# Row norms of an attention stage: sums of squares in four column tiles, and the factors spread by DMA instead of by TensorE

## The chip, the cores and the metric

The kernel runs on one core of a Trainium2 chip. The metric is device time in microseconds (us), first to last instruction of one execution, median of several. Five engines work side by side and each runs its own instructions in the order in which they were written: TensorE (PE; its weight loads stand in the trace as PEld), VectorE (DVE), ScalarE (ACT), GpSimd (POOL) and SyncE (SP). In this kernel SP issues every DMA, so a DMA that waits for its data holds back all DMAs written behind it. Matmul results land in PSUM, in banks of 512 fp32 values per partition.

## The reference

Three stages, fp32 throughout. For 8 batches, 8 heads, 576 tokens and head size 64:

```python
p_packed = sm_attn(p, k, v)              # 32 packed queries per head
out = sm_attn(q, p_packed, p_packed)     # 576 tokens per head over 32 packed rows
x = out.transpose(0, 2, 1, 3).reshape(4608, 512)

rms = np.sqrt(np.mean(x * x, axis=-1, keepdims=True) + 1e-06)
xn = x / rms * rms_g                     # the norm that the change is about
g = xn @ w_gate                          # 512 x 1536
silu = g * (1.0 / (1.0 + np.exp(-g)))
x = silu * (xn @ w_val) @ w_out          # 1536 x 512

h = (x @ w1) * (x @ w2) @ w3             # 512 x 1024, 1024 x 1024
return h @ w_out2                        # 1024 x 512
```

## The kernel before

The first 500 us hold the attention and the gated layer, batch by batch; the rest holds the output products, which the change doesn't touch.

**Attention.** `pack(b)` (line 182) makes the packed rows of a batch, `unpack(b)` (line 256) the second attention and the row norm. Neither multiplies its attention weights by the packed rows: what leaves `unpack` is `a2T`, the softmax weights with the 32 packed rows of four heads on the 128 partitions, two such halves `e`, and 576 tokens in the free dimension. The packed rows are folded into the gate and value weights instead (`wb_unit`, line 349). So the sum of squares of a token's output row is taken through the 32x32 Gram matrices `G` of the packed rows: `sq` = (G a2T) * a2T (lines 305 to 317), the halves added on POOL (line 319), and then summed over the 128 partitions. Lines 323 to 339 do that sum and what follows: five matmuls with `sq` as the stationary operand and a 128x2 tile of ones moving, so that tokens come out on partitions; one DVE instruction that scales it (`ssq`); two small POOL instructions (+1e-6, power -0.5, giving `rinv`, 128 partitions x 5); five TensorE transposes of `rinv`, each column repeated 128 times, which put the 576 factors on every partition; and two DVE products that scale `a2T` with them. `ah` and `al` are the high and low fp32r halves of the result, split by ACT (`ah`) and DVE (`al`).

**Dense units.** `dense_units(b)` (line 382) is the gated layer: 48 units for a batch, each of six matmuls of 288 tokens into one of four PSUM banks named `gv`. Units come in pairs. After the first of a pair ACT takes a tanh (`th`, line 402) and DVE a product (line 403), which frees the bank; after the second ACT copies the bank (`vl`, line 407, two buffers) and POOL multiplies (`ht`, line 408, three buffers). Every four units one `ht` is stored to `hT_d` by SP. After units 3, 11, 19, 27, 35 and 43 `wb_unit` makes the next folded weights in eight matmuls (line 358), which ACT and DVE split into `wbh` and `wbl` (lines 59, 60).

**What sets the order.** The schedule is manual: `planned` runs a batch's dense units and, after unit n, one step (up to a `yield`) of each other generator for each time that n stands in its list. While the units of batch b run, `UNPACK` places the 18 steps of `unpack(b+1)`, `PACK` the 7 steps of `pack(b+2)`, and a third list the conversions of 64-bit weights (`convert`, lines 115 to 121, and a 512 KB load each). All small products take their PSUM from two alternating slots named `at`. In this text a step of `unpack` is U1, U2, ..., a step of `pack` P1, P2, ...; U13 is the sum over partitions, U14 the two POOL instructions, U15 and U16 the two scalings, U17 and U18 the splits. P4 (line 219) is followed by the load of the next `v` (`vt`, 1 MB and 128 KB). `pack` runs beside the units of batches 0 to 5 and loads `vt` beside those of 0 to 4; `unpack` of batches 1 to 7 runs beside those of 0 to 6, and `unpack(0)` before the first unit.

Of the kernel before, what the change touches and what calls it, by code (L numbers as in the profile page):

```python
# [8 lines left out]
F32 = mybir.dt.float32  # L9
# [23 lines left out]
def packed_attention_swiglu_bilinear(ctx: ExitStack, tc, qT, kT, v, v_end, pT, rms_g, w_gv, w_out,  # L33
                                     w1, w2, w3T, w_out2, out):
    nc = tc.nc
# [16 lines left out]
    def slot(tag):  # L52
        return slots.tile([128, 2, 512], F32, tag=tag, name=tag, bufs=2)
# [8 lines left out]
    ident = const.tile([128, 128], F32, name="ident")  # L62
# [6 lines left out]
    att = att_ctx.enter_context(tc.tile_pool(name="att", bufs=1, side="left"))  # L69
# [95 lines left out]
    wgv = wraw.tile([128, NC, 2, DFF], F32, name="wgv")  # L165
    bdP1T = att.tile([128, 2, NC, 2, NP], F32, name="bdP1T")
    G = att.tile([128, 2, 2, NP], F32, name="G")
    mhalf = att.tile([128, R], F32, name="mhalf")
    ones = att.tile([128, 2], F32, name="ones")
    nc.gpsimd.memset(ones, 1.0)  # L170
    nc.gpsimd.memset(mhalf, -0.5)
    nc.gpsimd.memset(bdP1T, 0.0)
# [4 lines left out]
    def place(c, e):  # L177
        return 32 * ((c + e) % NC)

    def pack(b):  # L180
# [7 lines left out]
        for a in range(2):  # L188
            for c in range(NC):
                for e in range(2):  # L190
                    e0 = slice(64 * e, 64 * e + 64)
                    nc.tensor.matmul(ts[e][32 * c:32 * c + 32, a, :HALF], lhsT=pTs[e0, c, b],
                                     rhs=ks[e0, c, HALF * a:HALF * a + HALF],
                                     start=True, stop=True, tile_position=(64 * e, 32 * c))
# [60 lines left out]
    def unpack(b):  # L255
# [12 lines left out]
        for a, t in enumerate(ts):  # L268
            for c in range(NC):
                for e in range(2):  # L270
                    e0 = slice(64 * e, 64 * e + 64)
                    r = place(c, e)
                    nc.tensor.matmul(t[r:r + 32, e, :HALF], lhsT=bdP1T[e0, b % 2, c, e, :],
                                     rhs=qs[e0, c, HALF * a:HALF * a + HALF],
                                     start=True, stop=True, tile_position=(64 * e, r))
        for a, t in enumerate(ts):
            nc.vector.transpose(out=a2.rearrange("p e t n -> p e (t n)")[:, :, HALF * a:HALF * a + HALF],
                                in_=t[:, :, :HALF])
# [25 lines left out]
        sq = att.tile([128, 2, S], F32, tag="sq", name="sq")  # L304
        ts = [slot("at") for _ in range(2)]
        for a in range(2):
            for e in range(2):
                for c in range(NC):
                    r = place(c, e)
# [3 lines left out]
                                     rhs=x[:, HALF * a:HALF * a + HALF],  # L313
                                     start=True, stop=True, tile_position=(k, r))
        for e in range(2):
            nc.vector.tensor_tensor(out=halves(sq[:, e]), in0=ts[e][:, :, :HALF], in1=halves(a2T[:, e]),
                                    op=ALU.mult)
            yield
        nc.gpsimd.tensor_tensor(out=sq[:, 0], in0=sq[:, 0], in1=sq[:, 1], op=ALU.add)
        yield  # L320
        ssq = att.tile([128, R], F32, tag="ssq", name="ssq")
        rinv = att.tile([128, R], F32, tag="rinv", name="rinv")
        t = slot("at")
        for r in range(R):
            nc.tensor.matmul(t[:, 0, 2 * r:2 * r + 2], lhsT=sq[:, 0, T0[r]:T0[r] + 128], rhs=ones,  # L325
                             start=True, stop=True, skip_group_check=True)
        nc.vector.tensor_scalar(out=ssq, in0=t[:, 0, :2 * R].rearrange("p (r j) -> p r j", j=2)[:, :, 0],
                                scalar1=0.0, scalar2=1.0 / DM, op0=ALU.max, op1=ALU.mult)
        yield
        nc.gpsimd.tensor_scalar(out=ssq, in0=ssq, scalar1=1e-6, scalar2=None, op0=ALU.add)  # L330
        nc.gpsimd.tensor_tensor(out=rinv, in0=ssq, in1=mhalf, op=ALU.pow)
        yield

        t = slot("at").rearrange("p a n -> p (a n)")
        for r in range(R):
            nc.tensor.transpose(t[:, 64 + T0[r]:192 + T0[r]], rinv[:, r:r + 1].to_broadcast([128, 128]), ident)
        for e in range(2):
            nc.vector.tensor_tensor(out=a2T[:, e], in0=a2T[:, e], in1=t[:, 64:64 + S], op=ALU.mult)
            yield
        ah = dp.tile([128, 2, S], F32R, tag="ah", name="ah", bufs=2)  # L340
        al = dp.tile([128, 2, S], F32R, tag="al", name="al", bufs=2)
        for e in range(2):
# [139 lines left out]
    for n in range(16):  # L482
        r, c = GROUPS[n // 4]
        w, kk = ((w1, r), (w1, r + 2), (w2, r), (w2, r + 2))[n % 4]
        jobs.append((w[128 * kk:128 * kk + 128, 512 * c:512 * c + 512], w12_d[n]))
    ow = converting(jobs, out_weight)

    PACK = [7, 7, 16, 31, 32, 40, 43]
    UNPACK = [0, 1, 3, 4, 6, 11, 13, 15, 17, 24, 24, 25, 31, 32, 40, 41, 42, 44]
    for b in range(B - 1):  # L490
        others = [(UNPACK, unpack(b + 1))]
        if b + 2 < B:
            others.insert(0, (PACK, pack(b + 2)))
# [567 lines left out]
```

## Time and profile before

| | us |
|---|---|
| median of 3 runs | 1362.85 (1362.68 to 1364.24) |
| the profiled execution | 1364.01 |
| its span, first to last instruction | 1361.9 |
| PE busy in the span | 1310.4 (96%) |
| DVE, POOL, ACT busy | 846.9, 607.5, 571.9 |
| mean granted TensorE clock | 0.985 |

The profile says for each engine when an instruction ran, how long, and what ended the wait before it. A busy PE isn't proof of a full PE, since matmuls overlap. Two views tell more: the timeline, where the distance from one start to the next is the time an instruction takes up, and the list of waits, where an engine that sets the pace has next to none. The first 107 us are start-up; from there to 500 us the dense units follow each other.

### The profile page before, as it was taken

The numbers are of one execution on the slowest core, as the hardware profiler recorded it, in microseconds if no ns is written. First come the engines' busy times: TensorE is split into PE (matmuls) and PEld (weight loads), VectorE is DVE, ScalarE is ACT, GpSimd is POOL, SyncE is SP. The second block draws the span as 40 slices with busy tenths as digits, with TensorE's granted clock in tenths as the row PEclk, the third lists the DMA queues.
The fourth block names the chain that finished last, engine by engine and source line by source line (L and its number), as shares of the span: only waits on it lengthen the run. The fifth ranks groups of instructions, "written<-read, shape, count | busy, mean of one in ns | idle before, by whom it ended". The sixth has DMA issues, their size and how long they took to land.

```text
span 1361.9 us, 23336 instructions
## 1 busy us (share of the span) xinstructions
PE 1310.4 (96%) x8824; PEld 1108.8 (81%) x8824; DVE 846.9 (62%) x1284; ACT 571.9 (42%) x1093; POOL 607.5 (45%) x524
## 2 busy tenths in 40 slices
PE   4589999999999999999999999999999999999998
PEld 2367888788888888888888888888888888899998
DVE  5787676776766557736376564567468457557444
ACT  3465565566656665625244342025005103304113
POOL 2466555466556552212132123447345545535543
PEclk9589999999999999999999999999999999999999
DMA  8755656575353467744299984656755855787875
GB/s 328 289 176 167 232 188 241 175 239 165 121 176 127 155 198 253 238 131 135 84 348 369 344 295 176 249 208 212 279 194 206 277 207 195 247 316 254 280 268 188
DMA packets 88704, 304.01 MB, mean 223 GB/s; under 512 B 9872, under 2 KB 14992, under 8 KB 74384
## 3 DMA queue, kind: packets, MB, share of 16 engines
q1 hardware_dynamic: 88592, 302.52, 63.5%
q8 instruction: 69, 1.13, 0.3%
q14 instruction: 43, 0.35, 0.1%
HBM read 223.87 MB, written 76.55 MB: 221 GB/s over the span
## 4 chain that ended last, share of the span: by engine, by line
PE 84%; DVE 5%; POOL 2%; issue 2%; DMA 2%; ACT 1%; SPq 0%; ACTq 0%; DVEq 0%; POOLq 0%
PE gv L396 19%; PE gv L896 13%; PE at L896 13%; PE at L583 12%; PE gv L583 7%; PE gv L990 5%; PE at L990 5%; PE gv L684 3%; PE at L358 3%; POOL sl L60 1%; DVE c_t L118 1%; DVE wgv L119 1%; PE at L325 1%; DMA hT_d<-ht 1%; DVE th L403 1%
## 5 line engine op out<-in xcount | busy, mean ns | idle before, releaser
L408 POOL TENSOR_TENSOR ht<-th,vl 128x288 f32<-128x288 f32 x192 | 162.5, 854 | 122.4 <-ACT vl L407 47.4
L396 PE MATMUL gv<-ah,wbh 128*128 128x288 f32 x768 | 175.1, 309 | 2.9 <-ACT vl L407 2.4
L396 PE MATMUL gv<-ah,wbl 128*128 128x288 f32 x768 | 165.2, 296 | 2.3 <-DVE wbl L60 2.3
L396 PEld LDWEIGHTS gv<-ah,wbh 128*128 128x128 f32 x768 | 121.9, 190 | 54.2 <-issue 24.5
L396 PE MATMUL gv<-al,wbh 128*128 128x288 f32 x768 | 165.0, 296 | 0.0
L60 DVE TENSOR_TENSOR hl<-hr,hh 128x512 fp32r<-128x512 f32 x108 | 100.0, 933 | 78.8 <-ACT hh L59 76.7
L922 POOL TENSOR_TENSOR s<-uc 128x512 f32<-128x512 f32 (+1 forms) x40 | 48.9, 1223 | 217.9 <-DVE uc L878 217.9
L121 POOL TENSOR_TENSOR c_o<-c_o,c_y 128x512 int32<-128x512 int32 x52 | 70.8, 1361 | 152.4 <-DVE c_o L119 114.2
L896 PE MATMUL gv<-xh,w 128*128 128x512 f32 (+1 forms) x560 | 137.9, 368 | 0.0
L896 PE MATMUL at<-xh,w 128*128 128x512 f32 (+1 forms) x560 | 137.8, 368 | 0.0
L396 PEld LDWEIGHTS gv<-ah,wbl 128*128 128x128 f32 x768 | 123.7, 189 | 3.4 <-DVE wbl L60 3.3
L396 PEld LDWEIGHTS gv<-al,wbh 128*128 128x128 f32 x768 | 124.0, 189 | 0.0
L403 DVE SCALAR_TENSOR_TENSOR th<-th,gv 128x288 f32<-128x288 f32 x192 | 84.9, 444 | 59.8 <-ACT th L402 43.2
L59 ACT ACTIVATE hh<-hr 128x512 fp32r<-128x512 f32 x108 | 67.8, 630 | 117.3 <-PE at L583 61.1
L896 PEld LDWEIGHTS gv<-xh,w 128*128 128x128 f32 x560 | 102.6, 188 | 13.4
L407 ACT ACTIVATE vl<-gv 128x288 f32<-128x288 f32 x192 | 78.9, 411 | 82.1 <-PE gv L396 49.4
L896 PEld LDWEIGHTS at<-xh,w 128*128 128x128 f32 x560 | 102.5, 188 | 13.2
L583 PE MATMUL at<-hh,wo_l 128*128 128x512 f32 x288 | 112.2, 390 | 0.0
L583 PE MATMUL at<-hl,wo_h 128*128 128x512 f32 x288 | 112.2, 390 | 0.0
L583 PE MATMUL at<-hh,wo_h 128*128 128x512 f32 x288 | 112.2, 390 | 0.0
L402 ACT ACTIVATE th<-gv 128x288 f32<-128x288 f32 x192 | 79.2, 413 | 43.5 <-PE gv L396 41.6
L60 POOL TENSOR_TENSOR xl<-yi,xh 128x1024 fp32r<-128x1024 f32 (+1 forms) x20 | 55.1, 2757 | 71.7 <-ACT xh L59 47.8
(158 smaller groups left out, 2790.6 us busy)
## 6 DMA issues: line engine op xcount, KB each, us to landing
w<-ws_d SPq DMA_DIRECT2D x40, 1024.0 KB, 4.9
w<-w_d SPq DMA_DIRECT2D x35, 1024.0 KB, 4.8
w<-ws_d SPq DMA_DIRECT2D x40, 768.0 KB, 5.1
hT_d<-ht SPq DMA_DIRECT2D x96, 288.0 KB, 4.0
hr<-hT_d SPq DMA_DIRECT2D x108, 256.0 KB, 4.8
w<-in_w_gv_dram SPq DMA_DIRECT2D x24, 512.0 KB, 6.8
w<-in_w_out_dram SPq DMA_DIRECT2D x20, 512.0 KB, 6.1
q<-in_qT_dram SPq DMA_DIRECT2D x8, 1152.0 KB, 7.1
```

The costliest lines, as they stand in the source:

```text
L59: nc.scalar.activation(out=hi, in_=src, func=AF.Copy)
L60: eng_lo.tensor_tensor(out=lo, in0=src, in1=hi.bitcast(F32), op=ALU.subtract)
L121: nc.gpsimd.tensor_tensor(out=d, in0=d, in1=shape(y), op=ALU.add)
L396: nc.tensor.matmul(t[:, :HALF], lhsT=w[:, e, 256 * i + 128 * f:256 * i + 128 * f + 128], rhs=x[:, e, HALF * hf:HALF * hf + HALF], start=(n ...
L402: nc.scalar.activation(out=th, in_=t[:, :HALF], func=AF.Tanh, scale=0.5)
L403: nc.vector.scalar_tensor_tensor(out=th, in0=th, scalar=1.0, in1=t[:, :HALF], op0=ALU.add, op1=ALU.mult)
L407: nc.scalar.activation(out=vl, in_=t[:, :HALF], func=AF.Copy, scale=0.5)
L408: nc.gpsimd.tensor_tensor(out=ht[:, hf], in0=th, in1=vl, op=ALU.mult)
L583: nc.tensor.matmul(acc[m], lhsT=w[:, kk, 128 * m:128 * m + 128], rhs=x, start=(kk == 0 and a == 0), stop=(kk == NF - 1 and a == 2))
L896: nc.tensor.matmul(t, lhsT=wi[:, r, pos, a], rhs=x[:, j, r, :w], start=(start and at == 0), stop=(at == 5), skip_group_check=True)
L922: nc.gpsimd.tensor_tensor(out=s2, in0=u2, in1=c22, op=ALU.mult)
L990: nc.tensor.matmul(t, lhsT=wi[:, s, k, 128 * m:128 * m + 128], rhs=x, start=(j in (0, 5, 4, 3) and k == 0 and n == 0), stop=(k == 3 and n ...
```

## The change

For batches 1 to 7 the sum over partitions, the power and the spread are made in another way; batch 0 keeps the old code under `if b == 0`.

- The five matmuls with `sq` stationary become four with a 128x32 tile of ones stationary and 144 tokens of `sq` moving each. They are set side by side in the array's columns (`tile_position=(0, 32 * c)`) and write 32 equal rows each into one bank.
- DVE scales 128x144 values instead of 128x5 (`sums`). Four DMAs take one row of each group of 32 and lay it out on 24 partitions, 6 tokens each (`ssq`, 96x6).
- POOL's two instructions work on 96x6; a DMA stores the factors in DRAM (`rinv_d`), and another reads them back to all 128 partitions (`rb`, 128x576, in the buffer of `turned`). The five transposes are gone. The two scalings read `rb` from SBUF.
- `unpack` has 19 steps instead of 18 for these batches (the read of `rb` is one by itself), and the lists of places are new, for the conversions too.

```diff
-        t = slot("at")
-        for r in range(R):
-            nc.tensor.matmul(t[:, 0, 2 * r:2 * r + 2], lhsT=sq[:, 0, T0[r]:T0[r] + 128], rhs=ones,
-                             start=True, stop=True, skip_group_check=True)
...
-        t = slot("at").rearrange("p a n -> p (a n)")
-        for r in range(R):
-            nc.tensor.transpose(t[:, 64 + T0[r]:192 + T0[r]], rinv[:, r:r + 1].to_broadcast([128, 128]), ident)
-        for e in range(2):
-            nc.vector.tensor_tensor(out=a2T[:, e], in0=a2T[:, e], in1=t[:, 64:64 + S], op=ALU.mult)
-            yield
...
+            t = slot("at")
+            for c in range(4):
+                nc.tensor.matmul(t[32 * c:32 * c + 32, 0, :Q4], lhsT=ones, rhs=sq[:, 0, Q4 * c:Q4 * c + Q4],
+                                 start=True, stop=True, tile_position=(0, 32 * c), skip_group_check=True)
+            nc.vector.tensor_scalar(out=sums, in0=t[:, 0, :Q4], scalar1=0.0, scalar2=1.0 / DM, op0=ALU.max, op1=ALU.mult)
+            for c in range(4):
+                nc.sync.dma_start(out=ssq[24 * c:24 * c + 24], in_=sums[32 * c:32 * c + 1].rearrange("p (a n) -> p a n", n=6))
+            yield
+            nc.gpsimd.tensor_scalar(out=ssq, in0=ssq, scalar1=1e-6, scalar2=None, op0=ALU.add)
+            nc.gpsimd.tensor_tensor(out=rinv, in0=ssq, in1=mhalf[:96], op=ALU.pow)
+            nc.sync.dma_start(out=rinv_d[b], in_=rinv)
+            yield
+            nc.sync.dma_start(out=rb, in_=rinv_d[b].rearrange("p n -> (p n)").partition_broadcast(128))
+            yield
+            for e in range(2):
+                nc.vector.tensor_tensor(out=a2T[:, e], in0=a2T[:, e], in1=rb, op=ALU.mult)
+                yield
...
-    PACK = [7, 7, 16, 31, 32, 40, 43]
-    UNPACK = [0, 1, 3, 4, 6, 11, 13, 15, 17, 24, 24, 25, 31, 32, 40, 41, 42, 44]
+    PACK = [6, 7, 18, 32, 34, 41, 47]
+    UNPACK = [0, 0, 3, 3, 7, 12, 14, 17, 17, 25, 26, 26, 30, 32, 35, 40, 40, 40, 42]
...
-            others.append(([9, 20, 28, 35, 46], some(ow, 5)))
+            others.append(([8, 19, 22, 31, 44], some(ow, 5)))
```

New lines shift the old ones: line 396 (the dense matmuls) becomes 421, line 219 becomes 221, 403 becomes 428, 60 becomes 62. In the rows below a name is what an instruction writes, then what it reads; "x2" counts equal neighbours.

On PE, where the sum over partitions stands, in a batch before:

```order
L396 MATMUL gv<-ah,wbl 128x288 x2
L219 MATMUL at<-vt,a1T 32x64 x40
L325 MATMUL at<-ones,sq 128x2 x5
L396 MATMUL gv<-ah,wbh 128x288 x2
L396 MATMUL gv<-al,wbh 128x288 x2
```

and after (line 350 is the new sum):

```order
L421 MATMUL gv<-ah,wbl 128x288 x2
L350 MATMUL at<-sq,ones 32x144 x4
L421 MATMUL gv<-ah,wbh 128x288 x2
L421 MATMUL gv<-al,wbh 128x288 x2
L421 MATMUL gv<-ah,wbl 128x288 x2
L421 MATMUL gv<-ah,wbh 128x288 x2
L421 MATMUL gv<-al,wbh 128x288 x2
L421 MATMUL gv<-ah,wbl 128x288 x2
L221 MATMUL at<-vt,a1T 32x64 x40
L421 MATMUL gv<-ah,wbh 128x288 x2
```

The sum stood behind P4 without a dense unit between them; now two units lie between, and the sum comes first.

On SP, at the same place (`w` is a weight load, `vt` the next batch's v, `wo_d` a converted weight), before:

```order
L106 DMA w_1957<-in_w_out_dram 128x1024
L376 DMA hT_d<-ht 128x576
L97 DMA vt<-in_v_dram 128x2048
L98 DMA vt<-in_v_end_dram 64x512
L376 DMA hT_d<-ht 128x576
```

and after:

```order
L354 DMA ssq<-sums 24x1x6 x4
L108 DMA w_2015<-in_w_out_dram 128x1024
L99 DMA vt<-in_v_dram 128x2048
L100 DMA vt<-in_v_end_dram 64x512
L358 DMA rinv_d<-rinv 96x6
L401 DMA hT_d<-ht 128x576
L360 DMA rb<-rinv_d 128x576
L401 DMA hT_d<-ht 128x576
```

The six new DMAs stand around the weight load and the load of `vt`, with an `ht` store behind each of the last two.

On DVE, around the scaling of `a2T` (`bdP1T`, `gP1T` and `G` belong to `pack`), before:

```order
L235 COPY bdP1T<-at 64x4x32 x2
L237 TENSOR_TENSOR gP1T<-at,gT 128x128
L338 TENSOR_TENSOR a2T<-a2T,at 128x576 x2
L403 SCALAR_TENSOR_TENSOR th<-th,gv 128x288
L60 TENSOR_TENSOR al<-a2T,ah 128x576
L249 COPY G<-at 128x64
L60 TENSOR_TENSOR wbl<-at,wbh 128x1024
L403 SCALAR_TENSOR_TENSOR th<-th,gv 128x288
```

and after:

```order
L363 TENSOR_TENSOR a2T<-a2T,rb 128x576 x2
L62 TENSOR_TENSOR al<-a2T,ah 128x576
L237 COPY bdP1T<-at 64x4x32 x2
L239 TENSOR_TENSOR gP1T<-at,gT 128x128
L428 SCALAR_TENSOR_TENSOR th<-th,gv 128x288
L62 TENSOR_TENSOR al<-a2T,ah 128x576
L62 TENSOR_TENSOR wbl<-at,wbh 128x1024
L428 SCALAR_TENSOR_TENSOR th<-th,gv 128x288
L120 TENSOR_SCALAR c_t<-c_h 128x512
L121 SCALAR_TENSOR_TENSOR c_o<-c_h,c_t 128x512
L428 SCALAR_TENSOR_TENSOR th<-th,gv 128x288
L266 COPY G<-at 128x64
```

The first split and the copies of P6 now stand between the scaling and the next `th` product, and the copy of `G` (P7) has moved behind a weight's conversion.

## Rows read from the trace of the kernel before

**Rows 1.** The page, busy time, share and instructions; then the stage 272 to 327 us.

```profile
PE 1310.4 (96%) x8824; PEld 1108.8 (81%) x8824; DVE 846.9 (62%) x1284; ACT 571.9 (42%) x1093; POOL 607.5 (45%) x524
...
272.00:327.00 55.00, 54.11 (x603) 45.23 (x602) 40.35 (x75) 34.29 (x75) 33.31 (x37) 1.00 0.60 203
```

**Rows 2.** Waits of PE from 100 to 500 us: total, times, longest.

```profile
PE gv L396 <- DVE wbl L60: 2.3, 4, 0.9
```

**Rows 3.** Timeline of PE at P4 and the sum: start, us, line, [idle].

```profile
275.98 0.42 PE L396 MATMUL gv<-ah,wbl 128*128 128x288 f32 x2
276.33 1.32 PE L219 MATMUL at<-vt,a1T 128*32 128x64 f32 x80
277.58 1.28 PE L325 MATMUL at<-ones,sq 128*128 128x2 f32 x10
278.72 0.51 PE L396 MATMUL gv<-ah,wbh 128*128 128x288 f32 x2
279.07 0.43 PE L396 MATMUL gv<-al,wbh 128*128 128x288 f32 x2
```

**Rows 4.** The chain that ended last, 285 to 300 us: start, us, what.

```profile
284.95 2.40 PE gv L396 x18
287.34 0.11 PE at L231
287.45 0.55 PE at L336 x5
...
290.63 1.09 PE at L358 x16
...
295.88 1.13 PE at L273 x32
```

**Rows 5.** Timeline of PE around a product in small tiles (U1).

```profile
295.46 0.43 PE L396 MATMUL gv<-ah,wbl 128*128 128x288 f32 x2
295.81 1.20 PE L273 MATMUL at<-q,bdP1T 64*32 64x288 f32 x32
...
297.31 0.42 PE L396 MATMUL gv<-al,wbh 128*128 128x288 f32 x2
```

**Rows 6.** Timeline of DVE: U6 ahead of a split of weights.

```profile
256.48 0.75 DVE L289 TENSOR_REDUCE rs<-a 128x18 f32<-128x576 f32 x1
...
257.88 1.16 DVE L60 TENSOR_TENSOR wbl<-at,wbh 128x1024 fp32r<-128x1024 f32 x1
```

**Rows 7.** Timeline of DVE: the scaled sums; then the scaling and what follows.

```profile
278.90 0.17 DVE L327 TENSOR_SCALAR ssq<-at 128x5 f32<-128x5 f32 x1 [0.49 <-PE at L325]
...
287.89 0.45 DVE L403 SCALAR_TENSOR_TENSOR th<-th,gv 128x288 f32<-128x288 f32 x1 [1.12 <-ACT th L402]
...
289.07 1.41 DVE L338 TENSOR_TENSOR a2T<-a2T,at 128x576 f32<-128x576 f32 x2
...
290.76 0.75 DVE L60 TENSOR_TENSOR al<-a2T,ah 128x576 fp32r<-128x576 f32 x1
```

**Rows 8.** Timeline of POOL: a late store, and U14.

```profile
271.97 1.56 POOL L408 TENSOR_TENSOR ht<-th,vl 128x288 f32<-128x288 f32 x2 [2.63 <-DMA hT_d<-ht]
...
281.05 0.23 POOL L330 TENSOR_SCALAR ssq<-ssq 128x5 f32<-128x5 f32 x1
281.37 1.20 POOL L331 TENSOR_TENSOR rinv<-ssq,mhalf 128x5 f32<-128x5 f32 x1
```

**Rows 9.** Timeline of SP: a DMA from SBUF to SBUF.

```profile
262.75 0.53 SPq L300 DMA_DIRECT2D turned<-a2T  x1
```

**Rows 10.** DMA issues, KB each, us to landing: 262 us; 278; 278.6; 288 us.

```profile
turned<-a2T SPq DMA_DIRECT2D x1, 72.0 KB, 2.5
...
vt<-in_v_end_dram SPq DMA_DIRECT2D x1, 128.0 KB, 5.8
...
hT_d<-ht SPq DMA_DIRECT2D x1, 288.0 KB, 6.0
...
hT_d<-ht SPq DMA_DIRECT2D x1, 288.0 KB, 2.3
```

More of the change, by code (lines that the diff above doesn't have):

```diff
@@ L22 @@
 HALF = S // 2
+Q4 = S // 4
 DM = H * D
@@ L167, in packed_attention_swiglu_bilinear @@
     G = att.tile([128, 2, 2, NP], F32, name="G")
-    mhalf = att.tile([128, R], F32, name="mhalf")
-    ones = att.tile([128, 2], F32, name="ones")
+    mhalf = att.tile([128, 6], F32, name="mhalf")
+    ones = att.tile([128, 32], F32, name="ones")
     nc.gpsimd.memset(ones, 1.0)
@@ L320, in unpack @@
         yield
-        ssq = att.tile([128, R], F32, tag="ssq", name="ssq")
-        rinv = att.tile([128, R], F32, tag="rinv", name="rinv")
-        t = slot("at")
-        for r in range(R):
-            nc.tensor.matmul(t[:, 0, 2 * r:2 * r + 2], lhsT=sq[:, 0, T0[r]:T0[r] + 128], rhs=ones,
-                             start=True, stop=True, skip_group_check=True)
-        nc.vector.tensor_scalar(out=ssq, in0=t[:, 0, :2 * R].rearrange("p (r j) -> p r j", j=2)[:, :, 0],
-                                scalar1=0.0, scalar2=1.0 / DM, op0=ALU.max, op1=ALU.mult)
@@ L329, in unpack @@
-        yield
-        nc.gpsimd.tensor_scalar(out=ssq, in0=ssq, scalar1=1e-6, scalar2=None, op0=ALU.add)
-        nc.gpsimd.tensor_tensor(out=rinv, in0=ssq, in1=mhalf, op=ALU.pow)
-        yield
-        t = slot("at").rearrange("p a n -> p (a n)")
-        for r in range(R):
-            nc.tensor.transpose(t[:, 64 + T0[r]:192 + T0[r]], rinv[:, r:r + 1].to_broadcast([128, 128]), ident)
-        for e in range(2):
-            nc.vector.tensor_tensor(out=a2T[:, e], in0=a2T[:, e], in1=t[:, 64:64 + S], op=ALU.mult)
-            yield
+        if b == 0:
+            ssq = att.tile([128, R], F32, tag="ssq", name="ssq")
+            rinv = att.tile([128, R], F32, tag="rinv", name="rinv")
+            t = slot("at")
+            for r in range(R):
+                nc.tensor.matmul(t[:, 0, 2 * r:2 * r + 2], lhsT=sq[:, 0, T0[r]:T0[r] + 128], rhs=ones[:, :2],
+                                 start=True, stop=True, skip_group_check=True)
+            nc.vector.tensor_scalar(out=ssq, in0=t[:, 0, :2 * R].rearrange("p (r j) -> p r j", j=2)[:, :, 0],
+                                    scalar1=0.0, scalar2=1.0 / DM, op0=ALU.max, op1=ALU.mult)
+            yield
+            nc.gpsimd.tensor_scalar(out=ssq, in0=ssq, scalar1=1e-6, scalar2=None, op0=ALU.add)
+            nc.gpsimd.tensor_tensor(out=rinv, in0=ssq, in1=mhalf[:, :R], op=ALU.pow)
+            yield
+            t = slot("at").rearrange("p a n -> p (a n)")
+            for r in range(R):
+                nc.tensor.transpose(t[:, 64 + T0[r]:192 + T0[r]], rinv[:, r:r + 1].to_broadcast([128, 128]), ident)
+            for e in range(2):
+                nc.vector.tensor_tensor(out=a2T[:, e], in0=a2T[:, e], in1=t[:, 64:64 + S], op=ALU.mult)
+                yield
+        else:
+            rb = att.tile([128, S], F32, tag="turned", name="rb")
+            sums = att.tile([128, Q4], F32, tag="sums", name="sums")
+            ssq = att.tile([96, 6], F32, tag="ssq1", name="ssq")
+            rinv = att.tile([96, 6], F32, tag="rinv1", name="rinv")
+            t = slot("at")
+            for c in range(4):
[5 more added lines that the diff above has]
+            yield
+            nc.gpsimd.tensor_scalar(out=ssq, in0=ssq, scalar1=1e-6, scalar2=None, op0=ALU.add)
+            nc.gpsimd.tensor_tensor(out=rinv, in0=ssq, in1=mhalf[:96], op=ALU.pow)
+            nc.sync.dma_start(out=rinv_d[b], in_=rinv)
+            yield
+            nc.sync.dma_start(out=rb, in_=rinv_d[b].rearrange("p n -> (p n)").partition_broadcast(128))
+            yield
+            for e in range(2):
+                nc.vector.tensor_tensor(out=a2T[:, e], in0=a2T[:, e], in1=rb, op=ALU.mult)
+                yield
```

1 line of the change is left out of this document (added).

## The prediction

> **What bounds the kernel now.** I read the page first, then the stages, then the waits of PE. PE is busy for 96% of the span, and 54.11 of 55 us of a batch's dense units at full granted clock [rows 1]. That alone could be overlap, so the waits come next: from 100 to 500 us the longest sum of PE's waits is four waits of up to 0.9 us, 2.3 together, for a split of weights on DVE [rows 2]. In this stage PE issues one thing behind another, and an instruction that leaves PE's row shortens the kernel by the distance that it took up there. DVE, ACT and POOL each have a quarter of a batch or more free, but they wait for one another, and SP issues in order: they matter where they are late by more than the four banks let PE run ahead. A batch's `unpack` has to be through before the next batch's first unit.
>
> **PE's part.** Before, P4 and the sum stand together. From the dense pair ahead of them to the second pair behind lie 279.07 - 275.98 = 3.09 us [rows 3]; 18 dense matmuls take 2.40 us, so a pair takes 0.27 and a unit 0.80 [rows 4]. Two pairs off, the visit costs 3.09 - 0.53 = 2.56. The same sum around U1, a product in small tiles, gives 297.31 - 295.46 - 0.53 = 1.32 [rows 5], where the chain counts 1.13 for its matmuls [rows 4]: 0.2 goes into entering and leaving small tiles. P4 by itself (277.58 - 276.33 = 1.25, [rows 3]) should then cost 1.45, and the sum's removal brings 2.56 - 1.45 = 1.11. The transposes bring 0.55 [rows 4].
>
> Four matmuls with 144 tokens come in. The nearest row is P4: 40 matmuls of 64 columns in 32-column tiles of full height, 1.25 us, or 0.49 ns per column and matmul; 4 x 144 x 0.49 = 0.28 us, and 0.2 for entering and leaving, 0.48. Low bound 0.28 (no price for the change of tiles), high bound 1.3 (the four one after the other: P4's ten rounds of four would then be 0.125 each, 0.28 for 144 columns, four times, and 0.2). I take 0.48, since P4 has the same tiles. P7 moves from beside a weight product, which uses the same tiles, to a place by itself: +0.2 in six batches. P6, two units of other lists and P3 move without a change of tiles. So six batches gain 1.11 + 0.55 - 0.48 - 0.2 = 0.98, and batch 7, whose sum has no P4 beside it, 1.2: **7.1 us**.
>
> **The four waits of PE.** They come where `wbl` of the second weight product is late. On DVE U6 stands just ahead of it, 257.88 - 256.48 = 1.40 us [rows 6]. Its new place, 12 instead of 11, is behind the split, and 1.40 is more than the 0.9 that was missing. But U4 moves to 3, and units 19 and 22 now both have a conversion: new lateness of some tenths elsewhere. Of 2.3 I take **1.5 us**, with 0 and 2.3 as ends.
>
> **The way by DMA.** This is the disputed part. I count from the start of the new sum on PE, after unit 30.
>
> When is `rb` wanted? PE needs 0.48 for the sum, ten units at 0.80, 1.45 for P4 and 1.1 + 0.2 for the weight product after unit 35 [rows 4]: unit 40 ends at 11.2. Before, unit 40 ended at 287.34 [rows 4] and its `th` product at 287.89 + 0.45 = 288.34 [rows 7], 1.0 later. So DVE comes to the scaling at **12.2**.
>
> When is it there? `sums` stands behind the `th` product of unit 30, which ends at 1.0; the instruction itself is between 0.17 (five values, [rows 7]) and the 0.7 of 576: 1.25. A DMA from SBUF to SBUF keeps SP for 0.53 [rows 9], so the last of four starts at about 3.1; 72 KB landed 2.5 after the start [rows 10]: 5.6. POOL waits for it, then needs 281.37 + 1.20 - 281.05 = 1.52 [rows 8]: 7.2. Now SP issues the store of `rinv`. It has just issued a weight and `vt`, which waits for P4 and so starts at about 4.1. The second part of `vt` took 5.8 us and an `ht` store issued 0.6 later 6.0, while the same store took 2.3 with nothing ahead [rows 10]: what is issued behind `vt` lands behind it. That puts the store at 4.5 + 5.8 = 10.3, some tenths more with the weight ahead; I take 10.8. SP waits for that, issues `rb`, as many bytes as an `ht` store, and with 2.3 it lands at **13.1**. Ends: 11.8 with nothing ahead (7.2 + 2.3 + 2.3), and 10.8 + 6.0 = 16.8 if the queue is full again.
>
> So DVE waits 0.9 us for `rb` in the batches with `vt` beside them, five of seven; in the two others 11.8 is ahead of 12.2 and it waits for nothing. Who waits for DVE? From the scaling on it has 1.41 for the two products, 0.75 for `al`, 0.9 for P6's copies, 0.45 for `th` of unit 42, `al` again, 1.2 for `wbl` and 0.45 for `th` of unit 44 [rows 6, 7]: 5.9, so unit 44's bank is free at 18.1. PE wants it for the next batch's first unit, seven units, 1.3 for a weight product and about 0.5 for P6 and P7 after 11.2: 18.6. The copy of `G` a little later has about as much in hand for U1. With some tenths for hand-overs 0.3 is left, and of a wait of 0.9 PE loses 0.6: **3.0 us** in five batches.
>
> What stands behind SP's waits: the `ht` stores. One is late by the wait for POOL, one by the wait for the store of `rinv`. POOL then waits for a buffer, as it does now for up to 2.63 us [rows 8] without a wait of PE; I cost it at nothing, and some tenths per batch if the `vl` buffers run out. POOL's wait for `ssq`, 2 to 3 us, is covered in the same way. The longer `sums` is below 0.6 on DVE, which was idle for 0.49 there [rows 7]: nothing.
>
> **The sum.** -7.1 - 1.5 + 3.0 = -5.6 us. The profiled execution took 1364.01 (span 1361.9), so it would take 1358.4; it lies 1.2 above the median of 1362.85, and the predicted median is **1357.3**. What comes after 500 us only moves forward.
>
> **Rivals.**
> *The DMAs are hidden.* If the small store slips past `vt`, `rb` is there at 11.8 and DVE waits for nothing: -7.1 - 2.3 = 1353.5 at best. For it: the row of 2.3. Against it: 6.0 behind `vt` [both rows 10]. The Trainium skill (DMA: Bandwidth & Descriptors, Anatomy of one DMA) fits 2.0 us plus bytes over 436 GB/s to a DMA issued by GpSimd; an estimate by that gives 5.1 for `ssq`, 8.6 for the store and 11.4 for `rb`, which is this rival. The same page (Queues, rings and completion order) says that descriptors are consumed in ring order, which is what the 6.0 shows.
> *DVE stands at the scaling for long, and PE behind it.* The gains are 8.6 us; five batches eat them when PE loses 1.7 in each, that is from a wait of 2.0 or a landing of `rb` at 14.2. At 15.3 PE loses 2.8 in each: 14 - 8.6 = +5.4, or 1368. For it: each of the three legs of the way had a spread of some us in the rows, and they add up. Against it: it takes 1.1 us beyond my count. The skill's same page (Specifications) says that pieces under 512 bytes are read, changed and written back; here they are 24 bytes, no row has such pieces in a free queue, and the page would lean to this rival.
> *The four matmuls don't run side by side.* +0.84 x 7 = 5.9, which leaves the kernel where it was, 1363.2. P4's 0.49 ns per column speaks against it: U1, with eight tiles in place of four, has 1.13 us for 16 matmuls of 288 columns, half as much per column.
>
> **How the numbers follow.** Forecast 0.43 (0.37 of it faster), hidden 0.24, a longer wait 0.28 (half of it within the bound, the rest slower), serial matmuls 0.05. Faster by over 0.2% (below 1360.1, about what a measurement here can tell): 0.61; within: 0.22; slower: 0.17. The range of 1352 to 1365 leaves out the best end of the second case and the bad half of the third.
>
> **What would show it.** The new sum about 0.28 long on PE with 0.5 from dense to dense; no `wbl` wait after U6; in DVE's timeline a wait of the first scaling for the DMA of `rb`, about 1 us beside dense batches 0 to 4 and none in 5 and 6; PE's waits then at the first unit or U1 of the next batch. I am wrong if `rb` is late by 2 us or never, or if PE waits at another place, units 20 to 24 above all, where DVE now has two transposes, a copy and a conversion in a row.

## The result, and the profile of the changed kernel

The changed kernel takes 1383.3 us, median of four runs (1381.27 to 1386.7), the kernel before 1362.99 beside it (1362.68 to 1364.24): a ratio of 1.015, 95% interval 1.0128 to 1.0171. It is slower by 20 us where 5.6 us of gain were forecast, and above the predicted range of 1352 to 1365. The profiled execution took 1386.70 us, its span 1384.9, at a mean granted clock of 0.977.

First the page, and the stage that answers to [rows 1], in the same columns:

```profile
PE 1317.7 (95%) x8775; PEld 1108.0 (80%) x8775; DVE 847.0 (61%) x1284; ACT 570.4 (41%) x1093; POOL 608.8 (44%) x524
...
272.00:327.00 55.00, 51.12 (x562) 41.90 (x568) 35.59 (x69) 29.75 (x66) 28.57 (x31) 0.97 0.61 204
```

PE has 49 instructions less in the span, yet in 55 us of dense units it is busy for 51.1 us instead of 54.1, and its clock is below 1. DVE, ACT and POOL have less work in the same stretch too. So the dense stage runs slower, and the waits say where. From 100 to 500 us (total us, times, longest):

```profile
PE gv L421 <- ACT vl L432: 13.5, 8, 3.5
PE at L350 <- POOL sq L321: 3.7, 3, 2.0
...
DVE a2T L363 <- DMA rb<-rinv_d: 22.8, 7, 5.2
...
POOL ht L433 <- DMA hT_d<-ht: 43.7, 15, 5.1
```

The four `wbl` waits of [rows 2] are gone. In their place PE waits for ACT's copies of the banks, DVE stands 22.8 us for `rb`, and POOL stands twice as long as before for stored `ht` buffers (20.6 us in the same stretch of the kernel before).

PE's part came out as laid out. The timeline of PE at the new sum and at P4, the places of [rows 3] (start, us, line):

```profile
228.60 0.43 PE L421 MATMUL gv<-ah,wbl 128*128 128x288 f32 x2
228.95 0.45 PE L350 MATMUL at<-sq,ones 128*32 128x144 f32 x8
229.34 0.54 PE L421 MATMUL gv<-ah,wbh 128*128 128x288 f32 x2
229.71 0.43 PE L421 MATMUL gv<-al,wbh 128*128 128x288 f32 x2
...
230.77 0.43 PE L421 MATMUL gv<-ah,wbl 128*128 128x288 f32 x2
231.13 1.32 PE L221 MATMUL at<-vt,a1T 128*32 128x64 f32 x80
232.38 0.53 PE L421 MATMUL gv<-ah,wbh 128*128 128x288 f32 x2
232.75 0.43 PE L421 MATMUL gv<-al,wbh 128*128 128x288 f32 x2
```

The visit of the sum costs 229.71 - 228.60 - 0.53 = 0.58, P4 by itself 232.75 - 230.77 - 0.53 = 1.45. But the way by DMA came out long. The chain that ended last, in the same batch (start, us, what):

```profile
229.95 0.31 DVE sums L352
...
230.28 0.78 SPq L354
...
231.11 0.77 SPq L354
...
231.94 0.71 SPq L354
...
232.69 3.06 DMA ssq<-sums
...
235.93 0.24 POOL ssq L356
...
236.25 1.36 POOL rinv L357
...
237.63 4.48 DMA rinv_d<-rinv
...
242.12 4.04 DMA rb<-rinv_d
...
246.19 0.77 DVE a2T L363
```

From 230.28 to 246.16, 15.9 us, the chain holds 1.6 us of POOL; the rest is SP issuing and DMAs landing. What DVE, ACT and PE do at its end stands in their timelines (start, us, what, and in brackets the idle time before and what ended it):

```profile
240.78 0.45 DVE L428 SCALAR_TENSOR_TENSOR th<-th,gv 128x288 f32<-128x288 f32 x1 [1.08 <-ACT th L427]
246.19 1.43 DVE L363 TENSOR_TENSOR a2T<-a2T,rb 128x576 f32<-128x576 f32 x2 [4.95 <-DMA rb<-rinv_d]
```

```profile
246.98 0.68 ACT L61 ACTIVATE ah<-a2T 128x576 fp32r<-128x576 f32 x1 [6.30 <-DVE a2T L363]
247.57 0.39 ACT L432 ACTIVATE vl<-gv 128x288 f32<-128x288 f32 x1
```

```profile
244.32 0.42 PE L421 MATMUL gv<-ah,wbl 128*128 128x288 f32 x2
248.01 0.85 PE L421 MATMUL gv<-ah,wbh 128*128 128x288 f32 x2 [3.27 <-ACT vl L432]
```

DVE waits 4.95 us. ACT's split `ah` waits for DVE, and behind it in ACT's order stand the copies that free the banks, so PE, which fills its four banks meanwhile, stops for 3.27 us. From one U1 to the next lie 67.2 us beside batch 0 before and 54 to 56 beside the later ones; after it is 71.6, then 58.5, 60.1, 59.5 and 60.1, which are the five batches beside which `vt` is loaded, then 54.7. DVE's waits for `rb`, batch by batch of the dense units 0 to 6, are 3.7, 1.8, 5.0, 4.2, 5.2, 1.1 and 1.9 us; the rows above are of the third, one of the longest.

### The profile page after: what moved, and what is told of

Its sections match the earlier page's. It is cut to its first block, busy times and chain, and to the rows that moved or that the text cites. A ratio compares the mean times of both kernels' runs of the same rounds, so it can differ in the third digit from the quotient of the medians.

```text
span 1384.9 us, 23253 instructions
## 1 busy us (share of the span) xinstructions
PE 1317.7 (95%) x8775; PEld 1108.0 (80%) x8775; DVE 847.0 (61%) x1284; ACT 570.4 (41%) x1093; POOL 608.8 (44%) x524
## 4 chain that ended last, share of the span: by engine, by line
PE 77%; DMA 5%; POOL 5%; DVE 4%; issue 3%; ACT 2%; SPq 1%; POOLq 0%; ACTq 0%; DVEq 0%
PE at L608 14%; PE gv L421 13%; PE gv L921 12%; PE at L921 12%; PE gv L608 7%; PE gv L1015 5%; PE at L1015 5%; PE gv L709 3%; PE at L383 2%; DMA rinv_d<-rinv 2%; DMA rb<-rinv_d 2%; POOL sl L62 1%; DMA hT_d<-ht 1%; POOL ht L433 1%; PE at L194 1%
## 5 line engine op out<-in xcount | busy, mean ns | idle before, releaser
L421 PE MATMUL gv<-ah,wbh 128*128 128x288 f32 x768 | 181.6, 318 | 14.0 <-ACT vl L432 13.7
L421 PE MATMUL gv<-al,wbh 128*128 128x288 f32 x768 | 168.2, 301 | 0.0
L421 PE MATMUL gv<-ah,wbl 128*128 128x288 f32 x768 | 168.2, 301 | 0.0
L421 PEld LDWEIGHTS gv<-ah,wbl 128*128 128x128 f32 x768 | 126.7, 193 | 1.0 <-DVE wbl L62 0.9
L421 PEld LDWEIGHTS gv<-al,wbh 128*128 128x128 f32 x768 | 127.3, 194 | 0.0
L921 PEld LDWEIGHTS at<-xh,w 128*128 128x128 f32 x560 | 102.5, 188 | 13.2
L62 POOL TENSOR_TENSOR xl<-yi,xh 128x1024 fp32r<-128x1024 f32 (+1 forms) x20 | 55.2, 2759 | 71.6 <-ACT xh L61 71.4
```

What stands on the lines that cost most here:

```text
L62: eng_lo.tensor_tensor(out=lo, in0=src, in1=hi.bitcast(F32), op=ALU.subtract)
L421: nc.tensor.matmul(t[:, :HALF], lhsT=w[:, e, 256 * i + 128 * f:256 * i + 128 * f + 128], rhs=x[:, e, HALF * hf:HALF * hf + HALF], start=(n ...
L921: nc.tensor.matmul(t, lhsT=wi[:, r, pos, a], rhs=x[:, j, r, :w], start=(start and at == 0), stop=(at == 5), skip_group_check=True)
```

## The experiments

Each diff is against the changed kernel (the buffer of `before_ht4` is put into the kernel before). Each ratio is to the kernel before in runs beside it, with its 95% interval. The theory at the start was that the wait for `rb` costs nearly all; its rivals were that the new places cost it, and that the new sum does.

**The change taken apart.** In `no_wait` the factors no longer come by DMA from the sums: `rb` is loaded early from other data. The other instructions stay, the other five DMAs too.

```diff
+            nc.sync.dma_start(out=rb, in_=qT[b, 0, 0, :].partition_broadcast(128))
...
-            nc.sync.dma_start(out=rb, in_=rinv_d[b].rearrange("p n -> (p n)").partition_broadcast(128))
```

> The changed kernel, all its DMAs kept, but rb is read before the sum from 576 values of the input q instead of from the stored factors, so that nothing waits for the three DMAs in a row; the scaling then uses wrong factors. Theory 1 (DVE's wait of 22.8 us in all at the first scaling, and what follows it on ACT and PE, is the loss): the waits there go, PE runs at full clock in the dense stage, and the time is that of the sum in the prediction with its third term at zero, 1352 to 1358 us. Theory 2 (the new places of the steps cost the time: late ht stores, POOL's 43.7 us of waits for them, the conversions): it stays above 1372.

In `old_sum_new_places` all batches take the old code, at the new places.

```diff
-        if b == 0:
+        if b >= 0:
...
-    UNPACK = [0, 0, 3, 3, 7, 12, 14, 17, 17, 25, 26, 26, 30, 32, 35, 40, 40, 40, 42]
+    UNPACK = [0, 0, 3, 3, 7, 12, 14, 17, 17, 25, 26, 26, 30, 32, 40, 40, 40, 42]
```

> The old sum and transposes for every batch, with the new lists of places (without the one for the read of rb). Theory 1: within 4 us of the kernel before, 1359 to 1367 us. Theory 2: most of the 20 us is in the places, 1375 to 1385 us.

Measured: `no_wait` 1365.61 us, 1.0018 [1.0004, 1.0032]; `old_sum_new_places` 1373.18, 1.0064 [1.0048, 1.0079]; the kernel before 1364.04 beside both. Step by step: the new places with the old sum cost 1373.2 - 1364.0 = 9.1; the new sum then brings 1373.2 - 1365.6 = 7.6; the wait for `rb` costs (1383.3 - 1363.0) - (1365.6 - 1364.0) = 18.7. The last step takes away more than DVE's wait. In the changed kernel SP waits too, for the store of the factors, with an `ht` store behind it, and in `no_wait` it doesn't:

```profile
SPq L360 <- DMA rinv_d<-rinv: 19.8, 7, 5.0
```

POOL's waits for stored `ht` buffers fall by it from 43.7 us to 30.7. So the way to `rb`, with both waits, is the largest part, the new sum is a gain, and the places are a loss of their own that no theory had in this size.

**The way by DMA.** `vt_later` loads `vt` with P6 instead of after P4, so that it is no longer ahead of the store of `rinv`.

```diff
-        load_v(b + 1)
+        if b < 2:
+            load_v(b + 1)
...
+        if b >= 2:
+            load_v(b + 1)
```

> The changed kernel with the load of the next v issued at P6 instead of P4, behind rb on SP's queue instead of ahead of the store of the factors. If the queue behind vt makes the store slow (theory 1 in the form that the prediction had): the store of rinv lands in 2.3 to 3.5 us instead of 3.2 to 5.9 in the first five batches, DVE waits some 1.5 to 2 us less in each, and the time falls by 7 to 10 us, to 1373 to 1376. If the small pieces are slow by themselves: legs and time unchanged, 1380 to 1386.

Measured: 1370.46 us, 1.0049 [1.0034, 1.0064], 14 less than the changed kernel. Its waits, and its chain in the same batch:

```profile
DVE a2T L366 <- DMA rb<-rinv_d: 11.9, 7, 2.8
```

```profile
230.57 1.36 DMA rinv_d<-rinv
...
232.02 4.57 DMA rb<-rinv_d
```

The store of 2.2 KB lands in 1.36 us instead of 4.48: the queue behind `vt` was 3.1 us of that batch's wait. `rb` takes as long as before, 4.57, with no `vt` ahead of it, so `vt` isn't what makes it long. (An `ht` store was issued 1.1 us ahead of it here.)

`earlier` keeps `vt` where it was and moves the sum to unit 25 and the steps ahead of it forward, so that the DMAs have more time.

```diff
-    PACK = [6, 7, 18, 32, 34, 41, 47]
-    UNPACK = [0, 0, 3, 3, 7, 12, 14, 17, 17, 25, 26, 26, 30, 32, 35, 40, 40, 40, 42]
+    PACK = [6, 7, 18, 32, 34, 41, 46]
+    UNPACK = [0, 1, 3, 4, 6, 9, 10, 13, 14, 21, 22, 23, 25, 28, 30, 41, 42, 43, 45]
```

> The changed kernel with the steps of unpack placed earlier: the sum after unit 25 instead of 30, the store at 28, the read at 30, the scaling at 41 and 42 instead of 40, softmax steps drawn forward. Theory 1: rb lands 17.2 us after the sum starts beside a vt load and 14 without; the scaling comes 16 to 17.5 after it, so DVE waits for 0 to 1 us and the time is 1353 to 1360. Theory 2 or a new lateness of the softmax steps: PE waits elsewhere, 1365 or more.

Measured: 1437.08 us, 1.0527 [1.0506, 1.0548]. DVE no longer waits for `rb`, and the kernel is the slowest of all. Waits from 100 to 500 us:

```profile
PE at L350 <- POOL sq L321: 23.8, 6, 4.2
```

PE reaches the sum before POOL has added the halves. The sum can't be moved ahead by moving a list: what feeds it is late first. That the wait for `rb` is gone in a slow kernel tells nothing of its price.

**Old places, new sum.** `new_sum_old_places` has the lists of before with a place for the read of `rb`; `no_wait_old_places` is the same with `rb` read early from other data, as in `no_wait`; `vt_later_old_places` has `vt` with P6 and U10 to U15 one to three units earlier (22, 23, 23, 28, 30, 32). The diff of the first:

```diff
-    PACK = [6, 7, 18, 32, 34, 41, 47]
-    UNPACK = [0, 0, 3, 3, 7, 12, 14, 17, 17, 25, 26, 26, 30, 32, 35, 40, 40, 40, 42]
+    PACK = [7, 7, 16, 31, 32, 40, 43]
+    UNPACK = [0, 1, 3, 4, 6, 11, 13, 15, 17, 24, 24, 25, 31, 32, 35, 40, 41, 42, 44]
...
-            others.append(([8, 19, 22, 31, 44], some(ow, 5)))
+            others.append(([9, 20, 28, 35, 46], some(ow, 5)))
```

> The new sum, power and DMAs with the old lists of places, the read of rb after unit 35. The sum stands at 31, the scaling at 40 and 41, one unit nearer than in the changed kernel. If the wait for rb is the main loss: DVE waits 4 to 6 us in the batches with vt and the time is 1376 to 1390. If the places are the main loss: 1360 to 1368.

> The new sum without a wait for the factors (rb is read early from the input q, so the scaling uses wrong factors), with the old lists of places, the read of rb being the one step more. It isolates the first term of the prediction: if the new sum is worth 7 us on PE and the new places cost some 9 us by themselves (old_sum_new_places 1373 against 1364, no_wait 1366), this takes 1355 to 1359 us. If the new sum brings nothing by itself, or the DMAs on SP's queue cost as much through late ht stores, 1362 to 1368.

> An attempt at a better version: the new sum and DMAs, the load of vt at P6, the old lists of places for everything but the chain of the sum, which is drawn forward (G products at 22, POOL's addition at 23, sum at 28, store at 30, read at 32, scaling at 40 and 41 as before). In vt_later DVE still waited 1.7 us a batch with the sum at 30; two units and a weight product more between sum and scaling should leave 0 to 0.3. Expected 1355 to 1362; if the stores of ht behind SP's waits cost what the sum brings, 1363 to 1370.

Measured: 1383.46 us, 1.0137 [1.0119, 1.0155]; 1371.61, 1.0053 [1.0036, 1.007]; 1377.21, 1.0094 [1.0077, 1.0111]. So the new sum is as slow at the old places as at the new. Two of the old places are one unit apart, the sum (31) and POOL's two instructions (32), and POOL stands there for the `ssq` DMAs. The row of the waits of `no_wait_old_places`, and behind it DVE's of `vt_later_old_places`:

```profile
POOL ssq L357 <- DMA ssq<-sums: 27.6, 7, 6.2
```

```profile
DVE a2T L366 <- DMA rb<-rinv_d: 0.7, 1, 0.7
```

The latter, whose DVE hardly waits for `rb`, is still 13 us above the kernel before. Here the theory that the wait for `rb` is nearly all fell: something else costs 9 us and more at either set of places.

**The fourth `ht` buffer.** What these kernels share are POOL's waits for stored `ht` buffers, longer than in the kernel before. From 100 to 500 us, the kernel before, `old_sum_new_places` and `vt_later_old_places`:

```profile
POOL ht L408 <- DMA hT_d<-ht: 20.6, 10, 4.5
POOL ht L433 <- DMA hT_d<-ht: 29.8, 11, 3.8
POOL ht L436 <- DMA hT_d<-ht: 39.4, 19, 4.0
```

SP issues in order, so an `ht` store that stands behind a wait of SP is late by it. The new theory: late stores are the 9 us. It is tested by one more buffer, which changes no place and no wait of SP (where memory was short, `sums` went into the half of `sq` that is free by then).

```diff
-                ht = dp.tile([128, 2, HALF], F32, tag="ht", name="ht", bufs=3)
+                ht = dp.tile([128, 2, HALF], F32, tag="ht", name="ht", bufs=4)
```

> The old sum with the new places, with four ht buffers instead of three. If the 9 us of the new places come from ht stores that stand behind SP's waits, so that POOL waits for a buffer, ACT for POOL and PE for ACT: POOL's waits for hT_d fall from 29.8 us to under 10 and the time to 1362 to 1367. If they come from DVE's and ACT's order (steps in one unit, P1 and P7 by themselves): 1370 to 1374, unchanged.

> no_wait (rb read early from the input q, factors wrong) with four ht buffers and the sums in sq. Against old_sum_new_places_ht4 (1364.5), where PE had no wait left, it gives the bare worth of the new sum: 1356 to 1358.5 if it is the 7.1 us of the prediction; 1360 to 1364 if the DMAs on SP's queue and POOL's wait for the sums still cost what the sum brings.

> vt_later (1370.5) with four ht buffers; the scaled sums go into the used second half of sq to make room. If late ht stores cost PE time there (24.7 us of POOL's waits): 1361 to 1366. If what is left is the wait for rb (11.9 us) alone: 1368 to 1371.

> The kernel before with four ht buffers. Its POOL waited 19.8 us for ht stores in the dense stage, but PE hardly waited: 1361 to 1364 if PE's few waits there had other causes, as the rows say; 1357 or less if late stores cost it too.

> vt_later_old_places (1377.2), where DVE no longer waited for rb (0.7 us) but POOL for ht stores 38.1 us in all, with four ht buffers and the sums in sq. If SP's waits and the stores behind them are the whole loss there: 1355 to 1361, faster than the kernel before. If something else costs the time: above 1368.

| four `ht` buffers in | us | ratio to before | with three |
|---|---|---|---|
| the kernel before | 1362.32 | 0.9994 [0.9985, 1.0004] | 1 |
| `old_sum_new_places` | 1364.49 | 1.0009 [1.0, 1.0018] | 1.0064 |
| `no_wait` | 1356.98 | 0.9956 [0.9941, 0.9971] | 1.0018 |
| `vt_later_old_places` (`old_places_ht4`) | 1363.45 | 1.0004 [0.9995, 1.0014] | 1.0094 |
| `vt_later` | 1368.35 | 1.0044 [1.0029, 1.0059] | 1.0049 |

The buffer brings nothing in the kernel before, and 0.0055 to 0.009, 7.5 to 12 us, in the three next ones. In the four kernels behind the first row POOL's waits for stored buffers go down to between nothing and 5.9 us. So the loss by the places was late stores. What made them late wasn't tried, but only one of SP's waits ahead of a DMA grew by more than 2 us with the places, that of the `vt` load for P4, first in the kernel before, then in `old_sum_new_places`:

```profile
SPq L97 <- PE at L219: 21.0, 5, 6.4
SPq L99 <- PE at L221: 36.0, 5, 8.9
```

The new sum alone brings 1.0009 - 0.9956, 7.2 us. The stage 217 to 272 us of `no_wait_ht4` shows PE nearly without a gap:

```profile
217.00:272.00 55.00, 54.84 (x609) 44.72 (x608) 39.73 (x77) 33.88 (x75) 31.62 (x35) 1.00 0.63 214
```

`vt_later` gains nothing from the buffer, because it still waits for `rb`:

```profile
DVE a2T L366 <- DMA rb<-rinv_d: 14.0, 7, 3.0
```

It stands 1.0044 - 0.9956, or 12.0 us, above `no_wait_ht4`, for 14.0 us of DVE's waits. With three buffers the same pair of kernels differs by less, 1370.5 - 1365.6 = 4.9. In both pairs the place of `vt` differs too, so neither number is the wait's alone. That PE is held by late stores anyway with three buffers would explain the difference, but isn't shown by itself. The two losses overlap, and the 9.1 and 18.7 from above hold only in the order in which they were taken.

**The half clock.** Behind PE's stand of 3.27 us the granted clock is lower. Stretches after it in the changed kernel (the eighth column is the clock):

```profile
248.00:250.00 2.00, 1.99 (x8) 1.99 (x9) 1.97 (x6) 2.00 (x5) 1.04 (x2) 0.50 0.73 290
250.00:252.00 2.00, 2.00 (x10) 2.00 (x9) 2.00 (x4) 2.00 (x6) 0.95 (x1) 0.50 0.04 17
```

The chain shows what that does to 18 dense matmuls, 2.40 us in [rows 4]:

```profile
248.01 4.69 PE gv L421 x18
```

Is that a loss of its own? Two kernels give PE 20 spare matmuls at this place. In `fill_wait` they stand behind unit 44; in `fill_early` just ahead of P6's transpose, beside the dense units of batches 0 to 4. The diff of the second:

```diff
+        if 2 <= b <= 6:
+            x = res["a2n", b - 2][0]
+            for _ in range(20):
+                nc.tensor.matmul(t[:, 1, :HALF], lhsT=x[:, 0, :128], rhs=x[:, 0, :HALF],
+                                 start=True, stop=True, skip_group_check=True)
```

> The changed kernel with 20 matmuls more (288 columns, 2.7 us at full clock) after unit 44 of dense batches 0 to 4, into a bank that nobody reads, where PE otherwise stands for 3.3 us. If the clock that fell to half behind the wait (18 dense matmuls in 4.69 instead of 2.40 us) is a cost of its own: the granted clock stays at 1.00 there and the time falls by 2 us for each of five batches, to 1372 to 1376. If the half clock only fills time in which PE would wait for DVE again: 1380 to 1386, unchanged.

> The changed kernel with 20 idle matmuls (288 columns, 2.7 us at full clock) just ahead of P6's transpose after unit 41 of dense batches 0 to 4, into a bank half that nobody reads. They come before PE's wait of 3.3 us and wait for nothing themselves, so PE only comes later to the wait and stands for about 0.6 us. If the half clock behind the wait is a cost of its own: the granted clock stays near 1.00, and the time falls by about 2 us for each of five batches, to 1371 to 1377. If it only fills time in which PE would wait again for DVE: unchanged, 1380 to 1387.

`fill_wait` took 1407.81, 1.032 [1.03, 1.034], and says nothing of the clock: its tile was still to be read, and PE waited 18.4 us for DVE's reads. `fill_early` took 1385.74, 1.0168 [1.0151, 1.0185], where the changed kernel has 1.015 [1.0128, 1.0171]. Its stretch after the wait:

```profile
246.00:252.00 6.00, 5.50 (x62) 3.99 (x60) 5.61 (x11) 4.92 (x11) 2.28 (x2) 1.00 0.66 229
```

The clock is full, and the medians show no gain. The profiles show some, from the scaling to the next U1, first in the changed kernel (its scaling starts at 246.19), then in `fill_early`:

```profile
254.37 1.20 PE L275 MATMUL at<-q,bdP1T 64*32 64x288 f32 x32
```

```profile
246.28 1.43 DVE L368 TENSOR_TENSOR a2T<-a2T,rb 128x576 f32<-128x576 f32 x2 [3.87 <-DMA rb<-rinv_d]
252.92 1.30 PE L280 MATMUL at<-q,bdP1T 64*32 64x288 f32 x32
```

That is 8.2 us against 6.6. In the five batches together it is 37.4 against 33.0, a gain of 4.4, of which 2.1 are lost again from U1 to the next scaling. PE waits a little later for DVE (`th`, 2.2 us in four waits). So the half clock isn't free there, but it cost less than the 2 us a batch of the expectation, and since the spare matmuls take PE's time as well, its price isn't settled.

**A version that beats both.** Three kernels have `vt` with P6, four buffers, `sums` in `sq`, and the sum some units earlier: `sum_28_old_ht4` at the old places otherwise (diff), `sum_27_ht4` and `sum_28_new_ht4` with the changed kernel's `PACK` and the sum at 27 and 28 of `UNPACK`, `rb` at 33.

```diff
-    PACK = [6, 7, 18, 32, 34, 41, 47]
-    UNPACK = [0, 0, 3, 3, 7, 12, 14, 17, 17, 25, 26, 26, 30, 32, 35, 40, 40, 40, 42]
+    PACK = [7, 7, 16, 31, 32, 40, 43]
+    UNPACK = [0, 1, 3, 4, 6, 11, 13, 15, 17, 23, 24, 24, 28, 32, 33, 40, 41, 42, 44]
```

> The changed kernel with four ht buffers, vt loaded at P6, and the chain of the sum drawn forward three units (G products at 22, sum at 27, POOL's step at 32, read at 33, scaling still at 40). Sum to scaling is then 13 units and about 15 us; in vt_later_ht4, three units nearer, DVE waited 2 us a batch. So no wait for rb is left, and the time is that of no_wait_ht4, 1356 to 1360, faster than the kernel before. If the steps drawn forward make PE wait for POOL's addition or the transposed weights: 1362 to 1370.

> Four ht buffers, vt at P6, the old places for all but the sum: G products at 23, addition at 24, sum at 28, POOL's step at 32, read of rb at 33, scaling at 40 and 41. Against old_places_ht4 (1363.5) POOL comes to the sums two units later and need not wait for them, and PE needs no slot that is still being split. If the limits leave room: 1357 to 1361. If rb is late again or the copies of P6 and the splits at the end of a batch press: 1362 to 1366.

> The same with the new places: G products at 24, addition at 25, sum at 28, POOL's step at 32, read at 33, scaling at 40, conversions at 20 and 27 instead of 19 and 22. If the limits leave room: 1357 to 1361; if DVE waits about 1 us a batch for rb: 1362 to 1366.

Measured: `sum_27_ht4` 1375.42, 1.0089 [1.0072, 1.0105]; `sum_28_old_ht4` **1357.96**, 0.9962 [0.995, 0.9975]; `sum_28_new_ht4` 1362.05, 0.9991 [0.9982, 1.0001]. Rows of the waits, from 100 to 500 us, first of `sum_27_ht4`, then of `sum_28_old_ht4`:

```profile
PE at L353 <- POOL sq L324: 9.7, 7, 3.8
PE at L317 <- DVE wbl L62: 7.0, 7, 1.2
```

```profile
PE gv L424 <- DVE al L62: 1.7, 4, 0.5
PE gv L424 <- DVE wbl L62: 1.5, 4, 0.5
...
DVE a2T L366 <- DMA rb<-rinv_d: 5.8, 6, 1.7
```

At 27 PE waits for POOL's `sq`, as in `earlier`; at 28 and the old places for little. The faster kernel is 4.7 us below the kernel before and about 1 above the one without any wait for `rb`. Against `before_ht4`, which has the same buffer, it is 0.9994 - 0.9962, 4.4 us faster. So the new sum was worth taking, once its DMAs had time and its stores a buffer.

## Why the prediction was wrong

Two terms of the sum failed. The wait for `rb` stood in it with 3.0 us, from 0.9 us of DVE's waiting in each of five batches. DVE waited 1.8 to 5.2 us in these, which is the prediction's own sign of being wrong, and 1.1 and 1.9 in the other two; with what hangs on it the wait cost 18.7. The late stores stood in it at nothing, and the new places alone, with the old sum, cost 9.1 by them.

**PE's part was right.** Forecast 7.1 us; measured 7.6 with three buffers and 7.2 with four. Both are taken between two kernels at the new places, so they leave out the price of P7's move and the `wbl` waits. Both terms together were forecast at 8.6, and `no_wait_ht4` is 6.0 us faster than the kernel before (4.0 to 8.0). P4 by itself cost the 1.45 worked out, the sum 0.58 where 0.48 was taken: the bounds of 0.28 and 1.3 held, and the rival of serial matmuls is out, with 0.39 us from the sum's start to the next dense start.

**The `wbl` waits went, and the same places lost more.** No such wait is left, which was the 1.5 us. But the sentence on the `ht` stores, "I cost it at nothing", failed. [rows 8] showed POOL already up to 2.63 us late without a wait of PE. That the `vl` buffers could run out was named, at some tenths, but not how much more POOL could be late before they do. And only the stores behind the new DMAs were thought of: the places made the stores later without these DMAs, and that was 9.1 us with the old sum, undone by a fourth buffer.

**The wait for `rb` was the right mechanism with the wrong size.** Step by step, in us from the start of the sum (228.95):

| step | forecast | measured | by the row |
|---|---|---|---|
| `sums` done | 1.25 | 1.3 | 229.95 + 0.31 |
| last of four `ssq` DMAs starts | 3.1 | 3.7 | SP, 0.77 each instead of 0.53 |
| `ssq` landed | 5.6 | 6.8 | 3.06 instead of 2.5 |
| `rinv` ready | 7.2 | 8.7 | 236.25 + 1.36 |
| store landed | 10.8 | 13.2 | 4.48 instead of 3.6 |
| `rb` landed | 13.1 | 17.2 | 4.04 instead of 2.3 |
| DVE arrives | 12.2 | 12.3 | 240.78 + 0.45 |

DVE's arrival is within 0.1. Every leg of the DMA way is longer than forecast, and together they are 4.1 us longer. (The 3.1 of the second line was itself 0.3 above its terms, since 1.25 + 3 x 0.53 = 2.84.) The leg of `rb` has the largest part, 1.7: it was priced as an `ht` store with an empty queue, because it moves as many bytes, but it took 4.04, and 4.57 and 4.84 in the same batch of `vt_later` and `sum_28_old_ht4`, which have no `vt` ahead of it. The store behind `vt` has 0.9, and SP's issuing 0.5, since a small DMA was given the 0.53 of `turned` [rows 9]. That pieces of 24 bytes are slow was the fear of the prediction's second rival; their store landed in 1.36 us in `vt_later`. By the fit in the Trainium skill (DMA: Bandwidth & Descriptors, Anatomy of one DMA), which is for DMAs that GpSimd issues, the store would take 2.0 us and `rb` 2.7, estimates; the runs show 1.36 and 4.48 for the one, without and with `vt` ahead, and 4.04 or more for the other, so the measurement decides against it for these DMAs of SP. The upper end in the prediction, 16.8 "if the queue is full again", lies near the 17.2, but by luck: it put 3.7 us more on the leg of `rb`, where 1.7 were, and nothing on the others. The range left it out.

The rule for what follows, that PE loses the wait less 0.3, fits: for `vt_later_ht4`, 14.0 us in seven waits less 2.1 makes 11.9, and 12.0 were measured, but with some 3 us of noise that can't tell 0.3 from nothing. For the changed kernel it gives 22.8 - 2.1 = 20.7, measured 18.7 where stores are late too. The place was wrong: the prediction followed DVE to unit 44's bank and expected PE to stop at the next batch's first unit or U1, but ACT's `ah`, written ahead of its copies of the banks, stands with DVE and stops PE at once. And all seven batches wait, also the two without `vt`, by 1.1 and 1.9.

**The rival was the case.** "DVE stands at the scaling for long" was priced at 1368 for `rb` at 15.3. Priced at 17.2 (a wait of 5.0, a loss of 4.7 in five batches) it would have been 23.5 - 8.6 = +15. Of the other 5 us some 2 lie in the two batches without `vt`: from U1 on they are as long as before, where gains of 1.0 and 1.2 had been forecast. The rest lies in the five, which lose 22.6 us between their U1s in the profiled execution. The second of them loses 4.4 for a wait of 1.8, so the wait isn't all there; how it shares the loss with the late stores isn't settled, since they overlap.

## What to carry to other kernels

A chain of small DMAs between engines should be priced leg by leg at the slowest row that fits each, with what is queued ahead at that very moment, and then compared with the time to the consumer; here every leg was longer than forecast, and the sum came out above the upper end that had been thought of. Where one queue issues in order, a wait in it delays all stores behind it, and an extra buffer for the stored tile is the cheap test of whether that matters. When an engine is made to wait, look first at what stands behind the waiting instruction on the engines that wait for it: here a split on ACT held the copies that free TensorE's banks.

## What the hardware showed that was not expected

The time that SP needs to issue a DMA doesn't follow its bytes here. Rows of the changed kernel, with least, median and largest ns of one in all batches:

```profile
L354 SPq DMA_DIRECT2D ssq<-sums x28: 705/772/1093, 114.7 to 464.4; - x28
L358 SPq DMA_DIRECT2D rinv_d<-rinv x7: 326/332/347, 121.4 to 468.3; - x7
L360 SPq DMA_DIRECT2D rb<-rinv_d x7: 319/319/320, 124.6 to 469.8; - x7
```

A row of 576 bytes laid out on 24 partitions keeps SP for 0.77 us, the 2.2 KB of `rinv` for 0.33, and the 288 KB spread to all partitions for 0.32. The number of pieces isn't it either, since `ssq` is written to 24 partitions and `rinv` read from 96. The DMAs that stay within SBUF are the longer ones (`turned` takes 0.53 to 0.59 in both kernels); why isn't shown. The four DMAs of a batch together take 3.1 us of SP, in order.

The granted clock fell to 0.50 (1.2 GHz) after PE had stood for 3.3 us and stayed there until 254 us, 6 us after PE had gone on. A full clock in its place brought U1 nearer to the scaling by 0 to 1.5 us a batch in the profile, and nothing in the medians of `fill_early`.
